# Output matmuls of a linear-attention stage: 32-column strips replaced by a mix of 128, 64 and 32 columns

## The chip, the cores and the metric

The kernel runs on one core of a Trainium2 chip. The metric is the device time in microseconds of one execution. A core has five engines that run side by side: TensorE (matmul, PE in the profile, with its weight loads as PEld), VectorE (DVE), ScalarE (ACT), GpSimd (POOL) and SyncE (SP), and queues for DMA. A matmul holds a stationary operand (the weights, loaded by an instruction of its own) of up to 128 rows and 128 columns and streams the moving operand past it; each column of the stationary operand gives one partition of the result in PSUM. A matmul with 32 columns uses one 32-column strip of the array and writes 32 partitions.

## The reference

A linear attention with decay and a bonus for the present token runs over 4 batches, 8 heads, 768 tokens and a head size of 48; a two-layer network with a leaky ReLU follows on its 3072 x 384 result.

```python
def _attn_ref(r, k, v, w, u):                      # r, k, v: (4, 8, 768, 48)
    ...
    for t in range(S):
        kt, vt, rt = (k[:, :, t].copy(), v[:, :, t].copy(), r[:, :, t].copy())
        cur = np.einsum('bhd,bhe->bhde', u[None] * kt, vt)
        y[:, :, t] = np.einsum('bhd,bhde->bhe', rt, state + cur)
        state = w[None, :, :, None] * state + np.einsum('bhd,bhe->bhde', kt, vt)
    return y.astype(np.float32)

def _moe_ref(x, w_in, w_out):                      # x: (3072, 384), d_ff 2048
    h = x @ w_in
    g = np.maximum(0.01 * h, h)
    return (g @ w_out).astype(np.float32)
```

## The kernel before

The 3072 tokens are worked in 24 stages of 128 tokens, six for each batch. In a stage the attention is a masked product: scores between the 128 tokens (decay folded into two tables that multiply r and k), times v, plus r times the state that the earlier stages of the batch left. The eight heads are held as four pairs; a pair has 2 x 48 = 96 output dimensions.

The steps of a stage n, by the letters of the written order:
- P (`prep`): VectorE multiplies r and k by the tables into `qk`. From stage 8 on a DMA transposes them into `tp`; before that step T (`turn`, line 355) does it on TensorE.
- A (`a_mm`, line 377): TensorE makes the scores, with 48 rows, one matmul for each head, into two PSUM banks. M (`a_mask`, lines 387 and 391): VectorE masks them into `at`.
- The bonus for the token itself is a diagonal. In stages 0 to 7 (`DIAG` is 8) step Q (`prep2`, line 325) scales v into `vs`, and the outputs get it by a matmul of `vs` with the identity. Later it is put onto the diagonal of `at` ahead of the scores, on GpSimd.
- K and S (`kv_mm`, lines 404 to 413, and `state`): the state for the next stage, in `st`.
- Y (`y_part` with `y_mm`, line 493): the outputs, transposed, as 384 dimensions x 128 tokens in three slices of 128 partitions of one PSUM bank, which ScalarE copies to `xT` (line 508).
- G and J (`g1`, line 521, with 128 tokens; `g1_pair`, line 538, with 256): the first layer, and its leaky ReLU on ScalarE. H (`g2`, line 555): the second layer, then a copy (line 562) and a DMA to the output.

The first stages follow the list `ORDER`, written by hand, which gives every engine its instructions in that order. From stage pair 3 on a loop does it: for each pair it issues eight `g1_pair` (48 matmuls), the scores of two stages four ahead, the outputs of two stages, the states, and two `g2` (32 matmuls). Every engine works through its own list in order, and semaphores stand for the dependences that `Sched` finds; a step such as `y_mm` is one entry in TensorE's list, whatever number of matmuls it has.

Before the change `y_mm` takes the outputs in strips of 32 dimensions, twelve in all. Three strips make up a head pair, so the middle one belongs half to each head: `v_sb` holds every head in 64 columns, of which the last 16 are zero, and the middle strip is the sum of two matmuls with windows that reach into the zeros. A strip has one or two scored matmuls (`v_sb` with `at`), one with the state (`st` with `tp`) unless the stage is the first of a batch, and one with the diagonal (`vs` with `ident`) before stage 8. The four strips of a slice are interleaved, one matmul of each in turn.

Of the kernel before, what the change touches and what calls it, by code (L numbers as in the profile page):

```python
# [14 lines left out]
NC = S // L  # L15
NST = B * NC
HD = H * D
E = 64
# [3 lines left out]
NSL = HD // 128  # L22
# [15 lines left out]
class Sched:  # L38
# [8 lines left out]
    def add(self, eng, emit, R=(), W=(), dma=None):  # L47
        o = Op()
        o.eng, o.emit, o.dma, o.inc, o.val = eng, emit, dma, False, None
        deps = []  # L50
        for key in R:
            w = self.writer.get(key)
            if w is not None:
                deps.append((w, True))
        for key in W:
            w = self.writer.get(key)
            if w is not None:
                deps.append((w, False))
            for r in self.readers.get(key, ()):
                deps.append((r, False))  # L60
        o.deps = []
        for d, raw in deps:
            if d.dma is None and d.eng == eng and dma is None and (eng == "pe" or not raw):
                continue
            if d is not o and d not in o.deps:
                o.deps.append(d)
        for key in R:
            self.readers.setdefault(key, []).append(o)
        for key in W:
            self.writer[key] = o  # L70
            self.readers[key] = []
        self.ops.append(o)
        return o
# [47 lines left out]
def bass_rwkv5_eagle__then__act_leaky_relu_kernel(  # L121
# [13 lines left out]
    def SB(name, shape, dt=BF16):  # L135
        return ctx.enter_context(nc.sbuf_tensor(name, shape, dt))

    NQK, NTP, NVS, NAT, NT, NX, NG, NO = 6, 6, 6, 6, 6, 3, 3, 4
    TURNED, DIAG = 8, 8
# [4 lines left out]
    v_sb = SB("v_sb", [128, NST, H * E])  # L144
# [21 lines left out]
    ident = SB("ident", [128, 128])  # L166
# [4 lines left out]
    tp = [SB(f"tp{i}", [128, 2 * NP, 128]) for i in range(NTP)]  # L171
    vs = [SB(f"vs{i}", [128, HD]) for i in range(NVS)]
    at = [SB(f"at{i}", [128, 2, NP, 128]) for i in range(NAT)]
    st = [SB(f"st{i}", [128, NP, 2 * D]) for i in range(NT)]
# [6 lines left out]
    V, A, PE, SP, G = nc.vector, nc.scalar, nc.tensor, nc.sync, nc.gpsimd  # L181
# [284 lines left out]
    def y_mm(n, ps_y, key):  # L466
        it, ia, iv, is_ = n % NTP, n % NAT, n % NVS, n % NT

        def column(q):
            todo = []  # L470
            for s in range(NSL):
                p, kk = divmod(4 * s + q, 3)
                c0 = 128 * p
                one = []
                if kk < 2:
                    one.append((v_sb[:, n, c0 + 32 * kk:c0 + 32 * kk + 32], at[ia][:, 0, p, :]))
                if kk > 0:
                    c1 = c0 + 16 + 32 * kk
                    one.append((v_sb[:, n, c1:c1 + 32], at[ia][:, 1, p, :]))
                if n % NC:  # L480
                    one.append((st[is_][:, p, 32 * kk:32 * kk + 32], tp[it][:, p, :]))
                if n < DIAG:
                    one.append((vs[iv][:, 128 * s + 32 * q:128 * s + 32 * q + 32], ident[:, :]))
                todo += [(s, a, m, i == 0, i == len(one) - 1) for i, (a, m) in enumerate(one)]
            return todo

        def emit():
            columns = [column(q) for q in range(4)]
            for step in range(max(len(x) for x in columns)):
                for q in range(4):  # L490
                    if step < len(columns[q]):
                        s, a, m, first_mm, last_mm = columns[q][step]
                        last = PE.matmul(ps_y[32 * q:32 * q + 32, 128 * s:128 * s + 128], a, m,  # L493
                                         start=first_mm, stop=last_mm)
            return last

        reads = [("v", n), "v0", ("at", ia, 0), ("at", ia, 1), "ident", ("tp", it, 0)]
        if n < DIAG:
            reads.append(("vs", iv))
        if n % NC:  # L500
            reads.append(("st", is_))
        add("pe", emit, R=reads, W=[key])

    def y_part(n):
# [160 lines left out]
```

## Time and profile before

| | us |
|---|---|
| median of three timed runs | 173.73 |
| lowest and highest | 172.81, 174.05 |
| the profiled execution | 172.86 |
| its span, first to last instruction | 171.1 |
| TensorE busy (2195 matmuls, 2195 loads) | 164.0 |
| GpSimd, VectorE, ScalarE busy | 102.7, 95.6, 92.6 |

The span and all durations below come from one execution. Busy time of a group is the union of its instructions' lengths, so instructions that run side by side are counted once, while the mean is that of one. The column after the bar is the idle time of the engine ahead of the group. The lengths of matmuls are modelled in the profile; their starts are read here.

### The profile page before, as it was taken

How to read it: one execution, taken by the hardware profiler on the slowest of the kernel's cores; microseconds unless marked ns; L12 is line 12 of the kernel's file. 1: busy time of each engine (PE TensorE's matmuls, PEld its weight loads, DVE VectorE, ACT ScalarE, POOL GpSimd, SP SyncE). 2: the span in 40 equal slices, each digit the busy share in tenths (PEclk: the TensorE clock that was granted, in tenths of full speed). 3: DMA queues.
4: the chain of work that ended last, by engine and by line, in shares of the span. 5: the costliest groups of instructions: out<-in, count | busy, mean ns of one | idle time of the engine just before them, and what ended most of it. 6: DMA issues, size and time to landing. Idle time of an engine off the chain costs nothing.

```text
span 171.1 us, 5063 instructions
## 1 busy us (share of the span) xinstructions
PE 164.0 (96%) x2195; PEld 124.2 (73%) x2195; DVE 95.6 (56%) x209; ACT 92.6 (54%) x170; POOL 102.7 (60%) x117
## 2 busy tenths in 40 slices
PE   6799999969999999999999999999999999999994
PEld 1578898849666876876866867867868858768563
DVE  7699758733799959269289197197297430000000
ACT  4753888758313761952943934835816717629221
POOL 7999999990179999992992996956306300000000
PEclk9999999999999999999999999999999999999999
DMA  5999999999979999999599599899008011011022
GB/s 96 112 160 155 168 156 173 205 177 143 117 95 208 135 122 99 196 129 131 144 86 132 142 84 141 153 111 202 24 4 201 18 46 46 4 46 50 13 81 92
DMA packets 99114, 19.66 MB, mean 115 GB/s; under 512 B 92306, under 2 KB 99092, under 8 KB 99092
## 3 DMA queue, kind: packets, MB, share of 16 engines
q0 software_dynamic: 76512, 10.03, 90.0%
q1 hardware_dynamic: 21538, 9.11, 24.9%
q8 instruction: 17, 0.28, 0.6%
q10 hardware_dynamic: 1042, 0.20, 0.6%
q14 instruction: 5, 0.04, 0.1%
HBM read 20.45 MB, written 4.72 MB: 147 GB/s over the span
## 4 chain that ended last, share of the span: by engine, by line
PE 93%; POOL 3%; issue 2%; ACT 1%; POOLq 0%
PE ps L555 37%; PE ps L538 31%; PE ps L493 7%; PE ps L521 7%; PE ps L377 4%; PE ps L355 3%; PE ps L408 3%; POOL r_sb L210 1%; POOL k_sb L210 1%; ACT tp L366 1%; POOL v_sb L210 1%; PE ps L404 1%; PE ps L413 1%; POOL w_in_sb L220 0%; POOL ident L255 0%
## 5 line engine op out<-in xcount | busy, mean ns | idle before, releaser
L555 PE MATMUL ps<-w_out_sb,gT 128*128 128x384 bf16 (+2 forms) x400 | 64.6, 320 | 0.0
L538 PE MATMUL ps<-xT,w_in_sb 128*128 128x256 bf16 x480 | 54.5, 273 | 0.0
L555 PEld LDWEIGHTS ps<-w_out_sb,gT 128*128 128x128 bf16 x400 | 37.9, 98 | 22.7
L342 POOL TENSOR_TENSOR at<-ident,s_tok 128x512 bf16<-128x512 bf16 x32 | 33.8, 1080 | 30.2 <-DVE s_tok L334 30.2
L544 ACT ACTIVATE gT<-ps 128x512 bf16<-128x512 f32 x80 | 47.8, 597 | 7.2 <-PE ps L538 2.3
L538 PEld LDWEIGHTS ps<-xT,w_in_sb 128*128 128x128 bf16 x480 | 46.7, 98 | 6.4
L562 ACT ACTIVATE out_sb<-ps 128x384 f32<-128x384 f32 (+2 forms) x25 | 11.9, 478 | 54.6 <-PE ps L555 54.6
L391 DVE CAST_PREDICATED at<-mask,ps 128x512 bf16<-128x512 uint16 x32 | 19.9, 684 | 26.6 <-PE ps L377 26.6
L210 POOL DMA_DIRECT2D v_sb<-in_v_dram x24 | 22.5, 944 | 0.4 <-issue 0.4
L210 POOL DMA_DIRECT2D k_sb<-in_k_dram x23 | 21.6, 941 | 0.0
L210 POOL DMA_DIRECT2D r_sb<-in_r_dram x23 | 21.3, 928 | 0.0
L521 PE MATMUL ps<-xT,w_in_sb 128*128 128x128 bf16 x192 | 13.1, 225 | 0.2 <-issue 0.2
L508 ACT ACTIVATE xT<-ps 128x384 bf16<-128x384 f32 x24 | 11.0, 490 | 4.0 <-PE ps L493 3.6
L521 PEld LDWEIGHTS ps<-xT,w_in_sb 128*128 128x128 bf16 x192 | 11.8, 101 | 0.5 <-issue 0.2
L493 PE MATMUL ps<-at,v_sb 128*32 128x128 bf16 x384 | 12.1, 226 | 0.0
L526 ACT ACTIVATE gT<-ps 128x512 bf16<-128x512 f32 x16 | 9.6, 599 | 4.2 <-PE ps L521 3.7
L387 DVE TENSOR_TENSOR at<-ps,mask 128x512 bf16<-128x512 f32 x16 | 10.3, 683 | 2.0 <-PE ps L377 2.0
L332 DVE TENSOR_TENSOR rku<-r_sb,ku 128x384 bf16<-128x384 bf16 x16 | 10.8, 674 | 0.6
L493 PEld LDWEIGHTS ps<-at,v_sb 128*32 128x32 bf16 x384 | 9.3, 99 | 2.3 <-issue 0.5
L493 PE MATMUL ps<-tp,st 128*32 128x128 bf16 x240 | 10.3, 222 | 0.0
L366 ACT ACTIVATE tp<-ps 128x512 bf16<-128x512 f32 x15 | 8.2, 596 | 3.8 <-PE ps L355 3.8
L307 DVE TENSOR_TENSOR qk<-k_sb,ktab 128x384 bf16<-128x384 bf16 x23 | 9.8, 426 | 0.5 <-DMA k_sb<-in_k_dram 0.5
(62 smaller groups left out, 133.9 us busy)
## 6 DMA issues: line engine op xcount, KB each, us to landing
out_dram<-out_sb SPq DMA_DIRECT2D x23, 192.0 KB, 2.2
v_sb<-in_v_dram POOLq DMA_DIRECT2D x24, 96.0 KB, 5.7
r_sb<-in_r_dram POOLq DMA_DIRECT2D x23, 96.0 KB, 4.9
k_sb<-in_k_dram POOLq DMA_DIRECT2D x23, 96.0 KB, 4.6
w_in_sb<-in_moe_w_in_dram POOLq DMA_DIRECT2D x4, 384.0 KB, 7.4
w_out_sb<-in_moe_w_out_dram POOLq DMA_DIRECT2D x4, 384.0 KB, 10.4
tp<-qk SPq DMA_TRANSPOSE x16, 3.2
r_f<-in_r_dram SPq DMA_DIRECT2D x1, 192.0 KB, 3.5
```

Of the source, the lines that this page charges most:

```text
L210: add("pool", lambda: G.dma_start(dst, src), R=pace, W=[(which, n)], dma=f"{which}{n}")
L332: add("dve", lambda: V.tensor_tensor(rku[i2][:, :], r_of(n), ku[i2][:, :], ALU.mult), R=[("r", n), ("ku", i2)], W=[("rku", i2)])
L342: add("pool", lambda hh=hh, s_of=s_of: G.tensor_tensor(at[ia][:, hh, :, :], ident[:, :].unsqueeze(1).to_broadcast([128, NP, 128]), s_of.un ...
L387: add("dve", lambda hh=hh, part=part: V.tensor_tensor(at[n % NAT][:, hh, :, :], part, mask[:, :].unsqueeze(1).to_broadcast([128, NP, 128]) ...
L391: add("dve", lambda hh=hh, part=part: V.copy_predicated(at[n % NAT][:, hh, :, :], mask[:, :].bitcast(mybir.dt.uint16).unsqueeze(1).to_broa ...
L493: last = PE.matmul(ps_y[32 * q:32 * q + 32, 128 * s:128 * s + 128], a, m, start=first_mm, stop=last_mm)
L508: add("act", lambda: A.activation(xT[m % NX][:, :, 128 * half:128 * half + 128], ps_y[:, 0:HD].rearrange("p (s t) -> p s t", t=128), AF.Copy),
L521: last = PE.matmul(ps_g[:, 128 * f:128 * f + 128], w_in_sb[:, s, 128 * fb:128 * fb + 128], xT[ix][:, s, t], start=s == 0, stop=s == NSL - 1)
L538: last = PE.matmul(ps_g[:, 256 * f:256 * f + 256], w_in_sb[:, s, 128 * fb:128 * fb + 128], xT[ix][:, s, :], start=s == 0, stop=s == NSL - 1)
L544: add("act", lambda: A.activation(gT[ig][:, 2 * j:2 * j + 2, :].rearrange("p f t -> p (f t)"), ps_g[:, :], AF.Prelu, alpha=0.01), R=[key], ...
L555: last = PE.matmul(ps_o[:, 0:c1 - c0], gT[ig][:, s, 128 * half:128 * half + 128], w_out_sb[:, s, c0:c1], start=s == 0, stop=s == NFB - 1)
L562: add("act", lambda: A.activation(out_sb[io][:, c0:c1], ps_o[:, 0:c1 - c0], AF.Copy), R=[key], W=held)
```

## The change

`y_mm` writes the same sums with other pieces. The diagonal is added by three matmuls of 128 columns, one for each slice. Neighbouring strips that have the same moving operand are joined to 64 columns wherever they lie in one half of a slice. A stage of the first eight with a state now has 23 matmuls, a later one 20; without a state they are 15 and 12. The order is: diagonal first, then the state's pieces, then the scored ones, in the order of the slices, and last the four 32-column pieces of the middle strips and those next to them. The bookkeeping at the end sets the flags that start and stop an accumulation in each 32-partition row of the bank.

```diff
     def y_mm(n, ps_y, key):
         it, ia, iv, is_ = n % NTP, n % NAT, n % NVS, n % NT
 
-        def column(q):
+        def scored(h, dim, width, c0):
+            return dim, width, v_sb[:, n, E * h + c0:E * h + c0 + width], at[ia][:, h % 2, h // 2, :]
+
+        def carried(p, dim, width):
+            return dim, width, st[is_][:, p, dim - 96 * p:dim - 96 * p + width], tp[it][:, p, :]
+
+        def emit():
             todo = []
-            for s in range(NSL):
-                p, kk = divmod(4 * s + q, 3)
-                c0 = 128 * p
-                one = []
-                if kk < 2:
-                    one.append((v_sb[:, n, c0 + 32 * kk:c0 + 32 * kk + 32], at[ia][:, 0, p, :]))
-                if kk > 0:
-                    c1 = c0 + 16 + 32 * kk
-                    one.append((v_sb[:, n, c1:c1 + 32], at[ia][:, 1, p, :]))
-                if n % NC:
-                    one.append((st[is_][:, p, 32 * kk:32 * kk + 32], tp[it][:, p, :]))
-                if n < DIAG:
-                    one.append((vs[iv][:, 128 * s + 32 * q:128 * s + 32 * q + 32], ident[:, :]))
-                todo += [(s, a, m, i == 0, i == len(one) - 1) for i, (a, m) in enumerate(one)]
-            return todo
-
-        def emit():
-            columns = [column(q) for q in range(4)]
-            for step in range(max(len(x) for x in columns)):
-                for q in range(4):
-                    if step < len(columns[q]):
-                        s, a, m, first_mm, last_mm = columns[q][step]
-                        last = PE.matmul(ps_y[32 * q:32 * q + 32, 128 * s:128 * s + 128], a, m,
-                                         start=first_mm, stop=last_mm)
+            if n < DIAG:
+                todo += [(128 * s, 128, vs[iv][:, 128 * s:128 * s + 128], ident[:, :]) for s in range(NSL)]
+            if n % NC:
+                todo += [carried(0, 0, 64), carried(0, 64, 32), carried(1, 96, 32), carried(1, 128, 64),
+                         carried(2, 192, 64), carried(2, 256, 32), carried(3, 288, 32), carried(3, 320, 64)]
+            todo += [scored(0, 0, 64, 0), scored(1, 64, 32, 16), scored(2, 96, 32, 0),
+                     scored(3, 128, 64, -16), scored(4, 192, 64, 0),
+                     scored(5, 256, 32, 16), scored(6, 288, 32, 0), scored(7, 320, 64, -16),
+                     scored(1, 32, 32, -16), scored(2, 128, 32, 32), scored(5, 224, 32, -16), scored(6, 320, 32, 32)]
+            left = [(dim // 32 + j) % 4 for dim, width, *_ in todo for j in range(width // 32)]
+            begun = set()
+            for dim, width, a, m in todo:
+                s, row = divmod(dim, 128)
+                strips = set(range(row // 32, (row + width) // 32))
+                for j in range(width // 32):
+                    left.remove((dim // 32 + j) % 4)
+                last = PE.matmul(ps_y[row:row + width, 128 * s:128 * s + 128], a, m,
+                                 start=not strips & begun, stop=not strips & set(left))
+                assert strips <= begun or not strips & begun
+                begun |= strips
             return last
 
         reads = [("v", n), "v0", ("at", ia, 0), ("at", ia, 1), "ident", ("tp", it, 0)]
```

In `scored(h, dim, width, c0)` h is the head, dim the first output dimension, width the number of columns, and c0 the place in the 64 columns of that head. The list that the matmuls read, the banks, and the step's place in the order stay as they are.

## The prediction

> **What bounds the kernel now.** I read the page first, then the groups of instructions with shapes kept apart, then the timeline of TensorE around one output stage of the loop, then TensorE's waits. From the page:
>
> ```profile
> span 171.1 us, 5063 instructions
> ...
> PE 164.0 (96%) x2195; PEld 124.2 (73%) x2195; DVE 95.6 (56%) x209; ACT 92.6 (54%) x170; POOL 102.7 (60%) x117
> ...
> PEclk9999999999999999999999999999999999999999
> ...
> PE 93%; POOL 3%; issue 2%; ACT 1%; POOLq 0%
> ...
> L493 PE MATMUL ps<-at,v_sb 128*32 128x128 bf16 x384 | 12.1, 226 | 0.0
> ```
>
> TensorE is busy for 96% of the span, at full granted clock, and holds 93% of the chain that ended last. So a microsecond added to or taken from its instruction stream is one in the end time, nearly everywhere. Line 493, where the outputs are made, holds 7% of the chain, about 12 us: that is all that could be won. By shape:
>
> ```profile
> L493 PE MATMUL ps<-at,v_sb 128*32 128x128 bf16 x384 | 12.1, 226 | 0.0
> L493 PE MATMUL ps<-tp,st 128*32 128x128 bf16 x240 | 10.3, 222 | 0.0
> ...
> L493 PE MATMUL ps<-ident,vs 128*32 128x128 bf16 x96 | 5.2, 236 | 0.0
> ```
>
> These are 720 matmuls with 32 output columns and 128 streamed elements, 219 to 230 ns long each. But 720 x 0.22 us would be 158 us, so they overlap heavily. How, the timeline shows for the pair of stages at 110.7 us (56 matmuls; the columns are start, length, what):
>
> ```profile
> 104.83 5.40 PE L538 MATMUL ps<-xT,w_in_sb 128*128 128x256 bf16 x48
> 110.17 0.62 PE L377 MATMUL ps<-tp 48*128 48x128 bf16 x16
> 110.72 0.24 PE L493 MATMUL ps<-at,v_sb 128*32 128x128 bf16 x4
> ...
> 111.40 0.23 PE L493 MATMUL ps<-at,v_sb 128*32 128x128 bf16 x4
> 111.45 0.23 PE L493 MATMUL ps<-tp,st 128*32 128x128 bf16 x4
> 111.61 0.52 PE L408 MATMUL ps<-v_sb,qk 128*128 128x96 bf16 x8
> 111.96 0.33 PE L555 MATMUL ps<-w_out_sb,gT 128*128 128x384 bf16 x1
> ```
>
> Two readings carry the forecast. First, the matmuls start in **fours**: one for each 32-column strip, and the next four 0.05 to 0.06 us later. From 110.72 to 111.45 are 13 steps for 14 fours, 0.056 us each. A four is thus the price of one full-width matmul of 128 streamed elements. Second, **a change of shape costs extra**. The 16 matmuls of line 377 end at 110.17 + 0.62 = 110.79, so the last, 0.22 long, starts at 110.57; the first of line 493 starts at 110.72, 0.15 later, where 0.056 would have been the step. On leaving, the last four starts at 111.45 to 111.46 and line 408, full width again, at 111.61: 0.15 again. And line 538 ends at 110.23, its last (mean 0.273) starts at 109.96, and line 377 at 110.17: 0.21 where the step of 256 elements is 5.4/48 = 0.11. Three kinds of change, each some 0.09 to 0.10 us above the step.
>
> TensorE hardly waits for others:
>
> ```profile
> PE ps L408 <- issue: 1.7, 1, 1.7
> PE ps L247 <- DVE ones L239: 1.6, 1, 1.6
> PE ps L355 <- POOL ident L255: 1.0, 1, 1.0
> ```
>
> **What the change removes.** Stages before 8 that carry a state go from 40 matmuls to 23, those that carry none (0 and 6) from 28 to 15, later ones from 28 to 20, and 12 and 18 from 16 to 12: 6x40 + 2x28 + 14x28 + 2x16 = 720 become 6x23 + 2x15 + 14x20 + 2x12 = 472. That is 248 matmuls and 248 weight loads fewer. In array time it removes **nothing**: a 64-column matmul fills two strips and a 128-column one four. A loop stage is now 28 strip uses = 7 fours; afterwards its eight carried pieces fill 3 x 4 strips, its first eight scored pieces 3 x 4, the last four 4: 7 again. An early carried stage has 10 of each. Stages 0 and 6 have 7, 12 and 18 have 4, on both sides. Fewer instructions would pay only if issue set the pace; 0.056 us for four agrees with full-width matmuls of line 521, one at a time at 128 elements (the 60 that take 3.35 us in the chain), so the streaming sets it.
>
> **What it adds: changes of width inside a stage.** The new order in a carried stage is 64,32,32,64,64,32,32,64 (carried), 64,32,32,64,64,32,32,64, 32,32,32,32 (scored). Neighbours of equal width form 10 runs (64 | 32 32 | 64 64 | 32 32 | 64 64 | 32 32 | 64 64 | 32 32 | 64 | 32 32 32 32), each filling the array at most once. A stage without carried pieces has 6 runs. Before stage 8 three full-width matmuls stand ahead.
>
> The trace has no change between 64 and 32 columns, so I bound it. From below: 0 extra, when the strips that the next width takes are free, as the fours among themselves show (their starts lie within 0.01 us of each other). From above: the 0.15 us from start to start at every change of shape that the trace has, plus about 0.01 us because the first four after a change is slower (110.72 to the next at 110.78 or 110.79, 0.06 to 0.07). I take **0.15**, since full to 48 rows, 48 rows to 32 columns and 32 columns to full all come out alike: the price seems not to hang on which shapes they are.
>
> [...]
>
> The sum, between the full-width neighbours on either side, in us:
> - Loop pairs with both states carried (6 of them): 0.15 to enter + 20 runs x 0.15 = 3.15; now 0.15 + 0.74 + 0.15 = 1.04. +2.11 each, 12.7.
> - Pairs with stage 12 or 18 (2): 0.15 + 16 x 0.15 = 2.55; now 11 fours, 0.15 + 10 x 0.056 + 0.15 = 0.86. +1.69 each, 3.4.
> - Stages 1 to 3, alone: three full-width steps 0.17 without a change to enter, 0.15 to the first 64, 10 x 0.15: 1.82; now 0.15 + 9 x 0.056 + 0.15 = 0.80. +1.02 each, 3.1.
> - Stages 4 and 5 together: 3.64 against 0.30 + 19 x 0.056 = 1.36. +2.28.
> - Stages 6 and 7: 0.17 + 0.15 + 0.90, then 1.82, = 3.04 against 0.30 + 16 x 0.056 = 1.20. +1.84.
> - Stage 0: 1.22 against 0.30 + 6 x 0.056 = 0.64. +0.58.
>
> Together **+23.9**. Against it stands what the first stages already lose to waits (in the chain 0.87 us for stage 0 and 0.94 for stage 1): some 0.5 may be absorbed. The slower first four, 0.01 on about 220 runs, would add up to 2.2; I leave it to the range. The single 1.7 us "issue" stall, at 34.97 us, could move or go with 496 fewer instructions: 0 to -1.7, I take 0.
>
> **What hides it, and what is late next.** Nothing hides it: in the loop TensorE idles 0.0 before lines 538 and 555. ScalarE's copy (line 508) and so the next line 538 come later, but 5.2 us of line 555 stand between, so that costs nothing more. VectorE, ScalarE and GpSimd are at 54 to 60% and only gain room. No wait, DMA or order of steps is changed; an output step is still one entry with the same reads. The gaps are some 0.1 us each, so I expect no change of the granted clock.
>
> The profiled execution took 172.86 us (span 171.1, 1.8 around it), the three timed runs 172.81 to 174.05 with median 173.73, 0.9 more. 172.86 + 23.9 - 0.5 = 196.3; half of the 0.9 on top, rounded: **196.5 us**.
>
> **Rivals.**
> - *Forecast: every change of width stalls.* 194 to 200 us. For it: three kinds of change at one price. Against: in all of them the new shape overlaps the old one's strips. Chance 0.70.
> - *Only overlapping strips wait.* A 32-column piece in strips 2 and 3 would start at once beside a 64 in strips 0 and 1, and only a strip last used in another width would cost 0.15. Walking a loop stage in order, with 0.056 for equal and 0.15 for unequal, starts fall at 0, 0.06, 0.15, 0.20, 0.35, 0.41, 0.50, 0.56, 0.61, 0.70, and the next stage at 0.76 instead of 0.39: +0.37 a stage. With 0.28 for a mean stage of the pairs with 12 and 18, 0.18 for stage 0, 0.37 each for 1 to 3, 0.93 for 4 and 5, 0.75 for 6 and 7, the sum is 12 x 0.37 + 4 x 0.28 + 0.18 + 1.1 + 0.93 + 0.75 = 8.5: 172.86 + 8.5 + 0.4 = 182 us. Chance 0.13.
> - *The other side: 64 and 32 columns mix freely.* Then the fours stay fours and the place to look is line 493 in the loop, 1.04 a pair as now. What is left is the full-width diagonal: the change to enter is only moved behind it, and between stages 4 and 5 and 6 and 7 one more each way, 2 x 0.19 = +0.4, against 0 to -1.7 for the issue stall. 171.6 to 173.3, with the 0.4 of above 172 to 173.7: no slower. It decides as soon as a change between the two widths costs under about 0.01 us (224 runs x 0.01 = 2). For it: different strips now start within 0.01 us of each other. Against: nothing in the trace mixes shapes for free. Chance 0.15. [...]
> - Something else, as 64-column loads so slow that even this is exceeded: 0.02.
>
> **How the numbers follow.** The likeliest case gives 196.5, its own range 194 to 200 (the 2.2 of slower first fours above, the issue stall below). To leave out no more than 2 in 10 the range must take in the second case: 180 to 200. Within 1% is about what a measurement of this kernel can tell from no change. Faster needs free mixing and the issue stall gone: 0.02. The same: the rest of free mixing, 0.13. Slower: 0.85.
>
> **What would show it.** Right: in the changed kernel's timeline a loop pair of output stages takes 3.1 to 3.4 us from line 377 to line 408, starts step by 0.15 wherever the width changes, fewer than four matmuls run side by side, and the lines' other costs stay. If the pair takes 1.8, only overlapping strips wait; if 1.0, widths mix freely and the forecast is wrong. It is also wrong if the pair takes 3 us but the span grows by much less.

## The result and the profile after

| | before | after |
|---|---|---|
| median of four runs, the profiled one among them, us | 173.41 (172.81 to 174.05) | 201.88 (200.44 to 202.45) |
| profiled execution, us | 172.86 | 200.44 |
| its span, us | 171.1 | 198.7 |
| matmuls of line 493 | 720 | 472 |

The ratio is 1.163, with a 95% interval of 1.155 to 1.171: slower, as forecast, but by 28.5 us where 23 were forecast, and above the range, which ended at 200. Here and below, times are medians and ratios compare means of the fast executions; a single slow one, of the version with the diagonal of stages 2 and 3 (174.04 us at a clock of 0.990), is left out. The page after:

```profile
span 198.7 us, 4567 instructions
...
PE 193.3 (97%) x1947; PEld 138.7 (70%) x1947; DVE 95.9 (48%) x209; ACT 93.4 (47%) x170; POOL 102.7 (52%) x117
...
PEclk9999999999999999999999969999999999999999
...
PE ps L557 32%; PE ps L540 26%; PE ps L493 20%; PE ps L523 6%; PE ps L377 3%; PE ps L408 2%; PE ps L355 2%; POOL r_sb L210 1%; POOL k_sb L210 1%; DVE at L387 1%; ACT tp L366 1%; POOL v_sb L210 1%; PE ps L413 0%; PE ps L404 0%; POOL w_in_sb L220 0%
```

TensorE is as busy as before, with 248 matmuls fewer. Line 493 has grown from 7% of the chain to 20%. And one of the 40 digits of the granted clock is a 6: that was not there before. (Below line 493 the numbers are two higher than before: 557 is the second layer, 540 and 523 the first.) The groups of line 493, shapes kept apart:

```profile
L493 PE MATMUL ps<-at,v_sb 128*64 128x128 bf16 x96 | 17.8, 246 | 0.0
L493 PE MATMUL ps<-at,v_sb 128*32 128x128 bf16 x192 | 17.1, 233 | 0.0
L493 PE MATMUL ps<-tp,st 128*64 128x128 bf16 x80 | 14.6, 243 | 0.0
...
L493 PE MATMUL ps<-tp,st 128*32 128x128 bf16 x80 | 9.3, 230 | 0.0
...
L493 PE MATMUL ps<-ident,vs 128*128 128x128 bf16 x24 | 3.0, 239 | 0.1
```

A matmul has hardly become longer (means of 230 to 246 ns, where 222 to 236 were read before), but 16 pieces of 64 and 24 of 32 columns in a loop pair now cover over three microseconds. The timeline of TensorE shows it for the pair at 68.9 us:

```profile
68.88 0.92 PE L493 MATMUL ps<-tp,st 128*64 128x128 bf16 x8
69.56 1.09 PE L493 MATMUL ps<-at,v_sb 128*64 128x128 bf16 x12
70.58 0.92 PE L493 MATMUL ps<-tp,st 128*64 128x128 bf16 x8
71.26 1.09 PE L493 MATMUL ps<-at,v_sb 128*64 128x128 bf16 x12
72.28 0.30 PE L408 MATMUL ps<-v_sb,qk 128*128 128x96 bf16 x3
```

The view merges instructions of one line that overlap, under the first one's shape. Narrow windows of the same view take the second to the fourth run of one width apart:

```profile
69.05 0.23 PE L493 MATMUL ps<-tp,st 128*32 128x128 bf16 x2
...
69.22 0.25 PE L493 MATMUL ps<-tp,st 128*64 128x128 bf16 x2
...
69.39 0.23 PE L493 MATMUL ps<-tp,st 128*32 128x128 bf16 x2
```

The first run begins at 68.88 with one 64-column matmul on strips 0 and 1. The two 32-column ones that follow use strips 2 and 3, which were free, and yet start 0.17 later. So **every change of width stalls, wherever the strips are**: that rules out the rival in which only overlapping strips wait, and free mixing. By the trace's starts a step is 0.159 to 0.160 us from 32 to 64 columns and 0.173 to 0.174 from 64 to 32, where equal widths step by 0.056. The weight loads show what waits. Among equal widths before, a load of line 493 starts 0.054 us ahead of its matmul (median); at each of the 226 changes inside and into line 493 after, at most 0.004 us ahead. So at a change the next load is not started in advance. What else the array does in that time no run shows. From line 377's last start to line 408's first the pair takes 3.54 us, against 1.04 before.

Summed over the 14 groups of output stages in that way, from the start of the instruction ahead to the start of the one behind, the stages take 43.0 us where they took 14.7: **+28.2**. Add 1.4 for the clock (below), take off the one "issue" stall of 1.7 us, and 27.9 stands against a span that grew by 27.6.

### The profile page after: what moved, and what is told of

It reads as the page before. It is cut to its first block, busy times and chain, and to the rows that moved or that the text cites. A ratio compares the mean times of both kernels' runs of the same rounds, so it can differ in the third digit from the quotient of the medians.

```text
span 198.7 us, 4567 instructions
## 1 busy us (share of the span) xinstructions
PE 193.3 (97%) x1947; PEld 138.7 (70%) x1947; DVE 95.9 (48%) x209; ACT 93.4 (47%) x170; POOL 102.7 (52%) x117
## 4 chain that ended last, share of the span: by engine, by line
PE 94%; POOL 3%; DVE 1%; ACT 1%; issue 0%; POOLq 0%
PE ps L557 32%; PE ps L540 26%; PE ps L493 20%; PE ps L523 6%; PE ps L377 3%; PE ps L408 2%; PE ps L355 2%; POOL r_sb L210 1%; POOL k_sb L210 1%; DVE at L387 1%; ACT tp L366 1%; POOL v_sb L210 1%; PE ps L413 0%; PE ps L404 0%; POOL w_in_sb L220 0%
## 5 line engine op out<-in xcount | busy, mean ns | idle before, releaser
L557 PE MATMUL ps<-w_out_sb,gT 128*128 128x384 bf16 (+2 forms) x400 | 66.0, 324 | 0.0
L557 PEld LDWEIGHTS ps<-w_out_sb,gT 128*128 128x128 bf16 x400 | 38.4, 99 | 23.6 <-issue 1.5
L391 DVE CAST_PREDICATED at<-mask,ps 128x512 bf16<-128x512 uint16 x32 | 19.9, 686 | 36.7 <-PE ps L377 36.7
L493 PE MATMUL ps<-at,v_sb 128*32 128x128 bf16 (+1 forms) x288 | 26.6, 237 | 0.0
L510 ACT ACTIVATE xT<-ps 128x384 bf16<-128x384 f32 x24 | 11.8, 491 | 31.4 <-PE ps L493 31.4
L493 PEld LDWEIGHTS ps<-at,v_sb 128*32 128x32 bf16 (+1 forms) x288 | 14.9, 98 | 8.8 <-issue 0.2
L493 PE MATMUL ps<-tp,st 128*64 128x128 bf16 (+1 forms) x160 | 18.4, 236 | 0.0
L493 PEld LDWEIGHTS ps<-tp,st 128*64 128x64 bf16 (+1 forms) x160 | 10.2, 99 | 7.3 <-issue 0.2
```

What stands on the lines that cost most here:

```text
L391: add("dve", lambda hh=hh, part=part: V.copy_predicated(at[n % NAT][:, hh, :, :], mask[:, :].bitcast(mybir.dt.uint16).unsqueeze(1).to_broa ...
L493: last = PE.matmul(ps_y[row:row + width, 128 * s:128 * s + 128], a, m, start=not strips & begun, stop=not strips & set(left))
L510: add("act", lambda: A.activation(xT[m % NX][:, :, 128 * half:128 * half + 128], ps_y[:, 0:HD].rearrange("p (s t) -> p s t", t=128), AF.Copy),
L557: last = PE.matmul(ps_o[:, 0:c1 - c0], gT[ig][:, s, 128 * half:128 * half + 128], w_out_sb[:, s, c0:c1], start=s == 0, stop=s == NFB - 1)
```

## The experiments

All versions keep the changed kernel's `y_mm` and its sums. The edits stand behind the line that builds `todo`, unless said otherwise. Ratios are to the kernel before, run on the same chip.

**Is it the order, or the widths?** Every piece is cut back to 32 columns, in the new order:

```diff
+            todo = [(dim + 32 * j, 32, a[:, 32 * j:32 * j + 32], m)
+                    for dim, width, a, m in todo for j in range(width // 32)]
```

> The new order (diagonal, carried, scored, odd strips) with every piece cut back into 32-column matmuls: 720 matmuls again, no two widths in a stage, 28 changes of shape in all as before the change. Theory W (each change of width costs some 0.10 to 0.12 us above the step of 0.056): all of the loss is gone, ratio to before 0.99 to 1.005, a loop pair takes 1.04 us from line 377 to line 408. Rival O (the new order is at fault: pieces that add to the same strips follow too closely): still slow, ratio above 1.10. Rival S (64-column matmuls are slow in themselves): as W here.

172.62 us, ratio 1.0004 (0.998 to 1.003). A loop pair takes 1.04 us, all stages 14.8. The whole loss is gone with the mixed widths; order and accumulation cost nothing.

**One half of the change: only the diagonal in full width.**

```diff
+            joined = [(dim + 32 * j, 32, a[:, 32 * j:32 * j + 32], m)
+                      for dim, width, a, m in todo if width < 128 for j in range(width // 32)]
+            todo = [x for x in todo if x[1] == 128] + joined
```

> As the kernel with all pieces of 32 columns, but the diagonal of stages 0 to 7 in three full-width matmuls: one half of the change alone, 648 matmuls. W: 32 changes of shape instead of 28, four more at 0.10 us: +0.4 us against the all-32 version, ratio to before 0.99 to 1.01, and the loop as before. O: still slow, above 1.10. S: as W.

171.15 us, ratio 0.990 (0.987 to 0.994): **faster** by 1%, where 0.4 us more than the all-32 version had been expected. The stages 4 to 7, which hold the four added changes, do take 0.36 us more (3.14 against 2.78); all output stages take 14.9 us, 0.1 more, as stage 0 took 0.26 less. The gain is elsewhere, and TensorE's waits show where. In the all-32 version:

```profile
PE ps L247 <- DVE ones L239: 1.6, 1, 1.6
PE ps L408 <- issue: 1.4, 1, 1.4
PE ps L355 <- POOL ident L255: 1.0, 1, 1.0
PE ps L377 <- ACT tp L366: 0.2, 1, 0.2
PE ps L495 <- DVE vs L325: 0.2, 1, 0.2
```

and in this one:

```profile
PE ps L247 <- DVE ones L239: 1.6, 1, 1.6
PE ps L355 <- POOL ident L255: 1.0, 1, 1.0
PE ps L377 <- ACT tp L366: 0.2, 1, 0.2
```

The "issue" stall is gone; the changed kernel has lost it too. It is taken up again below.

**Are 64 columns slow, or the change to them?** The 472 matmuls of the changed kernel, sorted by width in each stage:

```diff
+            todo.sort(key=lambda x: -x[1])
```

> The same 472 matmuls as the changed kernel, but in each stage in the order of their width: 128, then 64, then 32 columns. W: 64 changes of shape instead of 240, a loop pair 1.5 us from line 377 to line 408 instead of 3.54, in sum +5.4 us against before: ratio 1.02 to 1.035, and 64-column matmuls follow each other in steps of 0.056 us. S (a step of 64 columns takes 0.16 whatever stands ahead): a loop pair has 8 such steps, 8 x 0.16 plus 6 x 0.056 and the entries, 2.0 us or more, ratio 1.06 or more. O: as the changed kernel, 1.16.

174.70 us, ratio 1.012 (1.008 to 1.016); the stages take 18.9 us, 4.1 more than with 32 columns alone. A loop pair in the timeline:

```profile
72.28 0.62 PE L377 MATMUL ps<-tp 48*128 48x128 bf16 x16
72.83 0.30 PE L494 MATMUL ps<-tp,st 128*64 128x128 bf16 x4
72.97 0.28 PE L494 MATMUL ps<-at,v_sb 128*64 128x128 bf16 x4
73.18 0.24 PE L494 MATMUL ps<-tp,st 128*32 128x128 bf16 x4
73.25 0.28 PE L494 MATMUL ps<-at,v_sb 128*32 128x128 bf16 x8
73.46 0.31 PE L494 MATMUL ps<-tp,st 128*64 128x128 bf16 x4
73.59 0.28 PE L494 MATMUL ps<-at,v_sb 128*64 128x128 bf16 x4
73.81 0.24 PE L494 MATMUL ps<-tp,st 128*32 128x128 bf16 x4
73.87 0.29 PE L494 MATMUL ps<-at,v_sb 128*32 128x128 bf16 x8
74.09 0.51 PE L408 MATMUL ps<-v_sb,qk 128*128 128x96 bf16 x8
```

Eight 64-column matmuls are through their starts in 0.20 us (72.83 to 73.03 by the trace): two at a time, in steps of about 0.056. Width itself is not slow. The pair takes 1.41 us. It has three changes more than before, 0.36 in all, 0.12 each. Expected were 1.50 and a ratio of 1.02 to 1.035. The pair comes out a little lower, and the rest of the difference is the lost "issue" stall, which the expectation did not count.

**Fewer changes still.** Odd stages run 32, 64, 128, so that a pair meets in one width:

```diff
+            if n % 2:
+                full = todo[:3] if n < DIAG else []
+                rest = [x for i, x in enumerate(todo[len(full):]) if i < 8 or x[1] == 32]
+                joined = [x for x in todo[len(full) + 8:] if x[1] == 64]
+                todo = [(dim + 32 * j, 32, a[:, 32 * j:32 * j + 32], m)
+                        for dim, width, a, m in rest for j in range(width // 32)] + joined + full
+            else:
+                todo.sort(key=lambda x: -x[1])
```

> Even stages in the order 128, 64, 32, odd stages 32, 64, 128 with the carried pieces of odd stages as 32-column matmuls, so that the two stages of a pair meet in one width. The same sums. W: 52 changes of shape, a loop pair 1.39 us, in sum +4.2 us against before: ratio 1.015 to 1.03, below the version that is only sorted by some 1.2 us. S: between 1.03 and 1.05, since odd stages keep four 64-column matmuls and even ones eight.

175.02 us, ratio 1.013 (1.009 to 1.018): a miss, not below the sorted version. The stages do come down, to 18.0 us and 1.29 a loop pair, by 0.9 us. That is less than the 1.2 expected because the kernel makes 55 changes, not 52: nine fewer than the sorted one, 0.09 to 0.10 us each. But in the profiled execution line 521's 12 matmuls ahead of stage 1 (numbered 531 and 524 in these two kernels) cost 0.7 us more than in the sorted version. This kernel first, then the sorted one:

```profile
14.25 1.49 PE L531 MATMUL ps<-xT,w_in_sb 128*128 128x128 bf16 x12
15.66 0.51 PE L501 MATMUL ps<-tp,st 128*32 128x128 bf16 x12
```

```profile
14.20 0.83 PE L524 MATMUL ps<-xT,w_in_sb 128*128 128x128 bf16 x12
15.01 0.34 PE L494 MATMUL ps<-ident,vs 128*128 128x128 bf16 x3
```

In the first they step by 0.107 us, in the second by 0.056: the steps are twice as long until about 16.2 us in the one and no longer in the other. (The row of the granted clock shows full speed there in both; this is read from the steps alone.) In the profiled executions that moment lies anywhere from before 14 to 17.7 us, so differences below 1 us between single executions of two kernels say nothing here.

**More changes, and the clock.** The 6 among the clock's digits after is a stretch at half speed from 115.76 to 119.17 us. By the windows view (stretch, length, busy times of the engines, then granted clock, DMA share and GB/s):

```profile
112.35:115.76 3.41, 3.41 (x48) 2.03 (x42) 2.48 (x4) 0.82 (x2) 2.94 (x4) 1.00 1.91 101
115.76:119.17 3.41, 3.41 (x19) 1.77 (x19) 2.58 (x8) 0.49 (x1) 0.00 (x0) 0.50 1.18 61
```

The 3.41 us ahead of it are almost exactly one pair of output stages. TensorE counts as busy there, but its array is thinly used: one step of 0.056 in each 0.16 to 0.17. Line 557's 32 matmuls behind it took 6.58 us in the chain, 5.20 after other pairs: 1.4 us lost. To see whether thin stretches cause it, the widths alternate piece by piece, 320 changes instead of 240, with pairs longer than those 3.41 us:

```diff
+            full, two, single = ([x for x in todo if x[1] == c] for c in (128, 64, 32))
+            second = next(i for i, x in enumerate(two) if x[0] % 128)
+            todo = full + [two.pop(second), two.pop(0)]
+            while two or single:
+                todo += single[:1] + two[:1]
+                single, two = single[1:], two[1:]
```

> The same 472 matmuls again, now with 64- and 32-column pieces in turn: 320 changes of shape instead of 240. Theory W (each change costs): a loop pair takes 4.9 us from line 377 to line 408 instead of 3.54, all output stages together 55.8 us against 43.0 in the changed kernel and 14.7 before; without any loss of clock some 212 us. Theory C (the granted clock falls to half for a 3.4 us window that lies wholly in the thin output stages): the pairs are now longer than such a window, about 45 in 100 of them hold one, some 3 to 4 in a run instead of 1, mean clock near 0.97 and another 4 to 6 us: 216 to 218. Rival to C (the fall to half clock comes at random): clock 0.98 to 1.00, 212 to 214 us.

227.29 us, ratio 1.312 (1.305 to 1.319), mean clock 0.932 to 0.939 in all four executions. A pair without a loss of clock takes 4.94 us, as theory W has it. The page and the windows view of this kernel:

```profile
PEclk9999999679999999958999958988999967999999
```

```profile
92.60:96.00 3.40, 3.40 (x29) 2.02 (x27) 2.25 (x4) 0.49 (x1) 1.75 (x2) 1.00 2.20 113
96.00:102.80 6.80, 6.80 (x36) 3.54 (x36) 4.39 (x12) 0.49 (x1) 0.61 (x1) 0.50 0.38 49
```

Five stretches at half clock, at 41.4, 96.0, 130.1, 150.6 and 181.3 us, begin in or at the end of a pair or of stages 4 and 5, with thin work in 3.0 to 3.4 of the 3.41 us ahead of each. Theory C's sign is right, its size too small: four of the five last 6.8 us, twice 3.41, so 30.7 us ran at half clock where some 12 were forecast (225 us x (1 - 0.932) x 2 = 31), and the time is 9 us above the 216 to 218. The five starts lie 54.61, 34.13, 20.48 and 30.72 us apart, which is 16, 10, 6 and 9 times 3.413. In the changed kernel's trace the record of the clock begins at 16.77 us, and the fall at 115.76 comes 29 times 3.413 later. So in each of the two traces the falls stand on a grid of 3.413 us, and it is a matter of phase whether a pair takes up a stretch of it almost whole: in the changed kernel the pair at 112.53 us does, in the stretch from 112.34 us.

The other direction: in the loop, 16 wide matmuls are put between the two stages of a pair.

```diff
-        for n in (2 * m + 2, 2 * m + 3):
-            if n < NST:
-                y_part(n)
+        if 2 * m + 2 < NST:
+            y_part(2 * m + 2)
+        g2(2 * m - 2)
+        if 2 * m + 3 < NST:
+            y_part(2 * m + 3)
...
-        g2(2 * m - 2)
         g2(2 * m - 1)
```

> The changed kernel, but in the loop one group of line 557 (16 wide matmuls, 2.6 us) stands between the two output stages of a pair. W: one change of shape more in each pair, 8 x 0.1 = +0.8 us. C: no thin stretch of the loop is longer than 1.9 us any more, so the clock stays at 1.000 there, and the runs lose the 1.4 us or more of each window; in sum 199 to 201 us against 200.4 to 202.5. Rival to C: clock between 0.98 and 1.00 as in the changed kernel, 201 to 203.5 us.

200.71 us, ratio 1.162 (1.156 to 1.168), clock 0.999 to 1.000 in all four executions, where the changed kernel has 0.983 to 0.991 in its four. The clock answers to the thin stretches, as C has it. But their length alone does not decide. In this version a whole stretch of the grid, 34.74 to 38.15 us, lies in stages 4 and 5, and the clock stays full. Counted afterwards over the traces that show the grid, in steps of 0.056 us (matmuls that run side by side count as one; 3.413 / 0.056 is 61), the six stretches at full clock that a fall follows hold 9 to 15.0 steps; the one of the changed kernel has the 15.0. The one just named holds 17.5, and every other stretch at full clock at least 15.2, in the changed kernel at least 23.5. No version was made to test that edge. The time can't tell the two kernels apart: the intervals overlap, and each pair has one change more.

**The gain of 1%: the "issue" stall.** Before, all 1.7 us fell ahead of the last matmul of a `kv_mm` near 36 us. Counted from 0 in the trace (weight loads, matmuls and semaphore waits in order of their starts), the instruction that waited is TensorE's number 1217, in the kernel before and in the all-32 version alike. The next version has all pieces in 32 columns but the diagonal of stages 2 and 3:

```diff
+            todo = [(dim, width, a, m) if width == 128 and n in (2, 3) else
+                    (dim + 32 * j, 32, a[:, 32 * j:32 * j + 32], m)
+                    for dim, width, a, m in todo
+                    for j in range(1 if width == 128 and n in (2, 3) else width // 32)]
```

> All pieces of 32 columns, but the diagonal of stages 2 and 3 alone in full width: 18 matmuls and 18 weight loads fewer, both ahead of the 1.4 to 1.7 us stall of line 408 near 36 us that the all-32 version and the kernel before have. Theory F (at that instruction TensorE has used up its instructions sooner than they are fetched): the same fetch now covers 36 more steps of the program, which from that place on take about 1.6 us, so the stall shrinks to 0 to 0.4 us and the time to 0.990 to 0.995 of before. Rival (the stall belongs to that place in the program or comes from something else): 1.4 to 1.9 us as before, ratio 0.998 to 1.003.

170.86 us, ratio 0.989 (0.985 to 0.993). Number 1217 waits again, but with 36 instructions fewer ahead it lies elsewhere in the program, in line 377, and the wait has shrunk to 0.2 us. The timeline of this version:

```profile
34.39 0.33 PE L408 MATMUL ps<-v_sb,qk 128*128 128x96 bf16 x4
34.56 1.47 PE L544 MATMUL ps<-xT,w_in_sb 128*128 128x256 bf16 x12
35.96 0.34 PE L377 MATMUL ps<-tp 48*128 48x128 bf16 x5
36.48 0.28 PE L377 MATMUL ps<-tp 48*128 48x128 bf16 x3 [0.18 <-issue]
```

The stall belongs to the count of instructions, not to a place in the program: it ends at 36.3 to 36.7 us in all three, whatever has been done by then. The shorter "issue" waits, of 0.2 to 0.3 us, bear this out. They fall at number 961, 256 instructions earlier, in each of the three kernels that have one: before the change in line 521, here and in the version with stages 0 to 3 (below) in line 497. The instruction queue on the two pages grows with the same count: 17 packets of 16 KB before (0.28 MB), 15 after (0.25 MB), for 4449 and 3953 instructions of TensorE, which is 262 and 264 for each packet. By the trace's DMA records the fourth of these packets runs from 34.10 to 35.05 us before, and TensorE goes on at 36.67. In all six waits it goes on 1.3 to 1.8 us after the end of such a packet. From the distance of 256 and these 262 and 264 it is an estimate that a packet brings some 256 instructions, and that TensorE had used up the earlier ones when it waited. What a packet holds, why it comes no sooner, and what fills the 1.3 to 1.8 us, no trace shows.

**Without the added changes.** Two ways to keep the fewer instructions and drop the extra changes of the diagonal. In the first, the diagonal stands last in stages 5 and 7:

```diff
+            joined = [(dim + 32 * j, 32, a[:, 32 * j:32 * j + 32], m)
+                      for dim, width, a, m in todo if width < 128 for j in range(width // 32)]
+            full = [x for x in todo if x[1] == 128]
+            todo = joined + full if n in (5, 7) else full + joined
```

> The version with only the diagonal in full width, but in stages 5 and 7 the diagonal stands last, so that stages 4 and 5 and 6 and 7 meet in 32 columns: 28 changes of shape instead of 32. W: 4 x 0.10 = 0.4 us less than that version (171.15 us), ratio to before 0.985 to 0.991. If changes cost nothing: as that version, 0.990.

170.98 us, ratio 0.988 (0.985 to 0.991). The expected 0.4 is too small a step for these runs, and was too high: behind stages 5 and 7 stands line 377 with its 48 rows, so leaving by full width is itself a change, and the kernel makes 30 changes, not 28. The stages 4 to 7 take 0.14 us less than in that version. In the second only stages 0 to 3 have the full-width diagonal (the edit of the version with stages 2 and 3, with `n < 4`):

> The diagonal in full width in stages 0 to 3 only, which stand alone between full-width or 48-row matmuls, so that no change of shape is added (28, as before); all else in 32 columns. 36 matmuls and 36 weight loads fewer than before, all ahead of the stall near 36 us. W with F: the output stages cost as before (14.7 to 14.9 us), the stall of 1.4 to 1.7 us is gone, with the shorter waits at its sides below 0.2 us: 0.985 to 0.99 of before. Without F: 0.998 to 1.003.

170.96 us, ratio 0.990 (0.985 to 0.994); the stages take 14.9 us, and one "issue" wait of 0.2 us is left. Four versions with some full-width diagonal thus lie at 0.988 to 0.990, faster than both kernels by an interval that excludes 1, and not to be told apart from each other.

## Why the prediction was right and wrong

**What bounds the kernel; no gain in array time.** Right. With equal widths 720 matmuls and 648 take 14.8 and 14.9 us in the output stages; the number of matmuls costs nothing there. That nothing hides the added time was right too: its terms come to 27.9 us, and the span grew by 27.6.

**Which rival.** Right: every change of width stalls. It was the forecast's main uncertainty, and the trace after settles it, since free strips wait too: a change between 64 and 32 columns takes 0.16 to 0.17 us from start to start, where equal widths step by 0.056. Why it takes that long no run shows.

**The term that was mis-sized: "I take 0.15".** It measured 0.160 into 64 columns, 0.173 to 0.174 out of them, and 0.162 from 32 columns to full. The trace before had only long stretches of one width, where the slowness of the first four falls on the second step. The prediction saw that as "about 0.01 us", added it up to 2.2, and left it out of the sum because most of it seemed a matter of range. But here nearly every run is a single four, so it is paid at each of the 224 runs; and it is 0.024 for 64 columns, which the trace before did not hold (lengths of 243 ns for the first 64-column matmul after a change, 229 to 230 for 32, 219 in mid-run). The mean of 0.160 and 0.174 is 0.017 above 0.15, and the matmuls of one run start 0.003 us apart, which the sum left out. Together a run takes 0.170 in a loop pair ((3.54 - 0.15) / 20), 0.020 above the forecast's price, and a pair 3.54 us where 3.1 to 3.4 was named as the sign of being right. 224 x 0.020 is 4.5 us: 23.9 becomes 28.4, of 28.2 measured. The terms for stages 4 and 5 and for 6 and 7 also count one full-width step twice, 0.06 us each.

**The waits that were to absorb 0.5 us.** They were misread. The 0.87 and 0.94 us of the chain are line 493's own pieces in stages 0 and 1: there the fours step by 0.107 us instead of 0.056, with no idle time between them, until 16.1 us. So there was nothing to absorb.

**"I expect no change of the granted clock."** Wrong: one stretch of 3.41 us at half speed cost 1.4 us in the profiled execution, and the clock was 0.983 to 0.991 in all four. The step looked at the length of a gap (0.1 us), where the length of the whole thin stretch mattered.

**The issue stall "could move or go": "0 to -1.7, I take 0".** It went, in this and in every version with at least 72 matmuls fewer, and all but went with 18 fewer. That row was treated as noise beside the forecast; by itself it decides the sign of the smaller versions.

**The range.** The errors are +4.3 (28.2 instead of 23.9), +0.5 for what was not absorbed, +1.4 and -1.7: together 4.5, where the profiled execution lies 4.1 above its sum of 196.3. The median lies another 1.4 above the profiled execution, of which the forecast had added 0.2. The upper end of 200 covered the 2.2 of the slower first fours and nothing for the clock.

## What to carry to other kernels

Count matmuls that share the array by how many strips are filled at a step and by how often the width changes from one to the next, not by their number: sorted by width, the same 472 matmuls cost 1% where they had cost 16%. Price a change from a run of one four, since the slowness of a run's first matmuls falls on the next step, and ask how long and how thinly TensorE is used: ahead of each of the six falls to half clock here stood 3.41 us with at most 15.0 steps of 0.056 us. And read a stall called "issue" in a dense early phase as a count of instructions: cutting 36 to 144 of them, at no saving of array time, gave the only gain.

## What the runs showed of the hardware that was not expected

- A change between 64 and 32 columns costs 0.10 to 0.12 us above a step even where the strips don't overlap, and the next weight load starts only with its matmul (at most 0.004 us ahead, 0.054 among equal widths).
- The first matmul after a change is, as the profile models it, 243 ns long with 64 columns, 229 to 230 with 32; in a run both have 219, and 64-column matmuls go two at a time in steps of about 0.056 us.
- The clock fell to half after 3.4 us of thin use in which the profile shows TensorE busy throughout, once in the changed kernel, five times and mostly for 6.8 us with 320 changes. The starts of the five lie 16, 10, 6 and 9 times 3.413 us apart, and each of the six falls follows 3.41 us with 9 to 15.0 steps of 0.056 us in them.
- TensorE stalled at its instruction number 1217, counted from 0, in three kernels, at two different places of the program, until 36.3 to 36.7 us, and more briefly, for 0.2 to 0.3 us, at number 961 in three. Each time it went on 1.3 to 1.8 us after a 16 KB packet of the instruction queue.
